# Windowed attention with a routed expert layer: transposing the probabilities in two row halves, and a new order of some loads and stores

## The chip, the cores and the metric

The kernel runs on one core of a Trainium2 chip. The core has four arithmetic engines that run side by side: TensorE (PE; its weight loads stand in a row of their own, PEld), VectorE (DVE), ScalarE (ACT) and GpSimd (POOL). SyncE (SP) only issues DMAs here. Sixteen DMA engines carry all transfers. The metric is the device time of one execution in microseconds (us); less is better. Times in the text are counted from the start of the profiled span.

## The reference

Attention in a window of 64 positions, over 8 batches, 8 heads, 576 positions and 64 dimensions a head, feeds a layer in which each token that passes a skip test goes through one of 8 experts:

```python
scores = q @ k.T / 8;  keep 0 <= i - j < 64, else -1e9
attn   = softmax(scores);  x = (attn @ v) as (4608, 512)
do     = x @ w_skip > 0;   e = argmax(x @ w_gate);  g = its softmax weight
out    = x;  out[do] = x + g * (relu(x @ w1[e]) @ w2[e])
```

## The kernel before

**Tiles.** The 4608 tokens are 36 tiles of 128, each made of two blocks of 64 positions. Nine tiles make a pair of batches: eight tiles with two neighbouring blocks of one batch, and a ninth, the tail tile, with the last block of either batch. For one tile TensorE writes 8 heads x 128 keys of scores into PSUM (`score`, line 252; line 238 adds the band mask). VectorE takes the row maximum and subtracts it (`lessen`, lines 267 and 268). ScalarE raises to e (`raise_e`, line 273) into s, 128 query rows by 8 x 128 keys. `transpose_p` turns each head's 128 x 128 probabilities over on TensorE (line 281), into two PSUM banks of four heads each, and ScalarE copies each bank into ptm (line 282). `av_tile` multiplies ptm by the values, their row sum and the gate columns (line 384). VectorE adds 1e-9 and takes the reciprocal (lines 395 and 396), scales into x (line 397) and into lh, the gate parts (line 403). In the last two tiles `into` hands `transpose_p` one score tile of two banks in place of two small ones.

**Order of the work.** The order on every engine is written by hand. Iteration t of the main loop issues, in this order: the loads due at t (`at`), the scores of tile t+1, gate matmuls (`gate_v`, line 331, which needs vT; `gate_vt`, line 339), `lessen` and `raise_e` of tile t, `tile_out` of tile t-2 (`av_tile` and its stores), `transpose_p` of tile t-1, and copies of values to the other half of the rows (`lower`). The routing of a group of 8 tiles (6 in two of them) is a generator, `route`, stepped by `routes` between those pieces. It puts small operations on GpSimd and VectorE, and matmuls (lines 513, 516 and 556) on TensorE, which may stand between a tile's value matmuls and its reciprocal. A score tile and the pt, pw and pk banks (tag "t") have two buffers, av has one, x has four.

**Queues.** SP issues loads and stores in program order, and a DMA takes one of eight semaphores in turn, so that an issue waits until the DMA eight before it has landed. `load_qk` (lines 210 and 211) brings the k and q of four tiles' worth of blocks, 1 MB, AHEADQ = 5 tiles ahead; `load_v` brings vT (line 292, 512 KB) and vm (line 298) AHEADV = 4 tiles ahead. `load_constants` (lines 176 and 177, 268 KB and 45 KB) is issued at the end of iteration 3, and `set_constants`, four small GpSimd operations that read them, at the end of iteration 5. A finished x is stored with a delay: `av_tile` appends it to `stores`, and `store` is called while more than SDELAY = 2 wait (in the last six tiles, while any waits). The store of an ordinary tile is one DMA of 128 rows (line 422); that of a tail tile is one DMA whose DRAM side has the shape 2 x 64 x 512 (line 425).

**After the loop** come the last transposes and value matmuls, mixed with the start of the expert layer. That layer is one long stream of float32r matmuls (lines 922 to 924), for which ScalarE and VectorE split the weights in a high and a low part (lines 848 and 852; the first three low parts on GpSimd). Tokens are gathered from and scattered to the output by indirect DMAs of GpSimd (lines 732 and 1025).

Of the kernel before, what the change touches and what calls it, by code (L numbers as in the profile page):

```python
# [8 lines left out]
F32 = mybir.dt.float32  # L9
# [9 lines left out]
B, H, S, HD = 8, 8, 576, 64  # L19
N, D, E, F = 4608, 512, 8, 1024  # L20
P = 128
NB = S // 64
NT = N // P
# [27 lines left out]
AHEADQ, AHEADV = 5, 4  # L51
SDELAY = 2
# [91 lines left out]
def window_attention_moe(ctx: ExitStack, tc, a, out):  # L144
    nc = tc.nc
# [6 lines left out]
    psum = ctx.enter_context(tc.tile_pool(name="psum", bufs=1, space=PSUM))  # L152
# [10 lines left out]
    ident = gid[:, 1]  # L163
# [67 lines left out]
    def score(t):  # L231

        ps = psc.tile([P, 2, 4, P], F32, name="ps")
        kinds = [min(i, 1) for _, i in tiles[t]]
        for hf in range(2):
            for r in range(2):
                h = slice(64 * r, 64 * r + 64)
                nc.tensor.matmul(
                    ps[64 * hf : 64 * hf + 64, r],
                    identb[h, h],  # L240
                    band[h, kinds[hf]].unsqueeze(1).to_broadcast([64, 4, P]),
                    start=True,
                    stop=False,
                    skip_group_check=True,
                )
        win = windows(t)
        for p in range(4):
            for hf in range(2):
                for r in range(2):
                    h = slice(64 * r, 64 * r + 64)  # L250
                    q, k = win[hf]
                    nc.tensor.matmul(  # L252
                        ps[64 * hf : 64 * hf + 64, r, p],
                        q[h, p],
                        k[h, :, p],
                        start=False,
                        stop=p == 3,
                        skip_group_check=True,
                    )
        ss[t] = ps  # L260

    def lessen(t):
        ps = ss[t]
        s = sp.tile([P, 2 * 4, P], F32, name="s")
        flat = ps.rearrange("p r h k -> p (r h) k")
        mx = sm.tile([P, 8], F32, name="mx", bufs=2)
        nc.vector.tensor_reduce(mx, flat, axis=AX.X, op=ALU.max)  # L267
        pace[0] = nc.vector.tensor_tensor(s, flat, mx.unsqueeze(2).to_broadcast([P, 8, P]), op=ALU.subtract)  # L268
        ss[t] = s

    def raise_e(t):
        s = ss[t]
        nc.scalar.activation(s, s, AF.Exp, scale=0.125)  # L273

    def transpose_p(t, into=None):
        s = ss.pop(t)
        ptm = ptp.tile([P, 8, P], F32, name="ptm")
        for r in range(2):
            pt = into[:, r] if into is not None else psum.tile([P, 4, P], F32, name="pt", tag="t", bufs=2)
            for p in range(4):  # L280
                nc.tensor.transpose(pt[:, p], s[:, 4 * r + p], ident)  # L281
            nc.scalar.copy(ptm[:, 4 * r : 4 * r + 4], pt)  # L282
        pts[t] = ptm

    ss, pts, vs = {}, {}, {}
# [32 lines left out]
    def keep_busy(n):  # L318

        idle = pav.tile([P, 2, 512], F32, name="av")  # L320
        for _ in range(n):
            nc.tensor.matmul(
                idle[:, 0], onesb, onesb.unsqueeze(1).to_broadcast([P, 4, P]),
                start=True, stop=True, skip_group_check=True,
            )
# [49 lines left out]
    def av_tile(t, lh, sums, av=None):  # L375
        blks = tiles[t]
        ptm, win = pts.pop(t), vs.pop(t)
        x = xp.tile([P, D], F32, name="x", bufs=XPB)
        if av is None:
            av = pav.tile([P, 2, 512], F32, name="av")  # L380
        banks["av"] = av
        for h in range(8):
            for hf in range(2):
                nc.tensor.matmul(  # L384
                    av[64 * hf : 64 * hf + 64, h // 4, (h % 4) * VW : (h % 4 + 1) * VW],
                    ptm[:, (h % 2) * 4 + h // 2, 64 * hf : 64 * hf + 64],
                    win[hf][:, h],
                    start=True,
                    stop=True,
                )  # L390
        if sums:
            sums()
        r = sm.tile([P, 2, 4], F32, name="r")
        src = av[:, :, : 4 * VW].rearrange("p z (h c) -> p z h c", c=VW)
        nc.vector.tensor_scalar(r, src[..., 64], 1e-9, None, op0=ALU.add)
        nc.vector.reciprocal(r, r)
        pace[0] = nc.vector.tensor_tensor(
            x.rearrange("p (z h c) -> p z h c", z=2, c=64),
            src[..., 0:64],
            r.unsqueeze(3).to_broadcast([P, 2, 4, 64]),  # L400
            op=ALU.mult,
        )
        nc.vector.tensor_tensor(  # L403
            lh.rearrange("p c (z h) -> p z h c", z=2),
            src[..., 65:74],
            r.unsqueeze(3).to_broadcast([P, 2, 4, 9]),
            op=ALU.mult,
        )
        if sums:
            sums()  # L410
        stores.append((x, blks))
        while len(stores) > (SDELAY if t < NT - 6 else 0):
            store()

    stores = []

    def store():
        x, ((b0, i0), (b1, i1)) = stores.pop(0)
        r0 = b0 * S + i0 * 64
        r1 = b1 * S + i1 * 64  # L420
        if r1 == r0 + 64:
            nc.sync.dma_start(out[r0 : r0 + P], x)
        else:
            both = out.rearrange("(b s) d -> b s d", s=S)[b0 : b1 + 1, i0 * 64 : i0 * 64 + 64]
            nc.sync.dma_start(both, x)

    def vector_part(t0, n, lh):
        lg = sm.tile([P, n, 9], F32, name="lg")
# [285 lines left out]
    def drip():  # L714
        if side:
            job = side.pop(0)
            if job:
                job[0](*job[1:])
# [28 lines left out]
    def clear_rows():  # L747
        for x in xgs:
            nc.gpsimd.memset(x, 0.0)
# [15 lines left out]
    def routes(n):  # L765

        for _ in range(n):
            for queue, h in ((late, held), (later, held2)):
                if not queue:
                    continue  # L770
                if h[0] in ("sums", "lists"):
                    h[1] += 1
                    if progress[0] < NT or h[1] < HOLD[h[0]] + (h is held2 and len(late)):
                        continue
                step(queue, h)

    def sums():
        step(late, held)
# [360 lines left out]
    first_of = [9 * (n // 4) + 2 * (n % 4) for n in range(NG)]  # L1139
    with tc.manual_schedule():  # L1140
# [16 lines left out]
        def when_at(t, f, n):  # L1157
            at.setdefault(max(t, 0), []).append((f, n))

        gate_at, lower_at, after_at = {}, {}, {}  # L1160
        for n in range(NG):
            if n >= 2:
                if n > 2:
                    when_at(first_of[n] - AHEADQ, load_qk, n)
                when_at(first_of[n] - AHEADV, load_v, n)
            gt = first_of[n] + 1 if n < 2 else first_of[n] - (2 if n > NSLOW else n == NSLOW)
            gate_at.setdefault(gt, []).append((gate_v, n))
            (after_at if n == 1 else gate_at).setdefault(gt + (n != 1), []).append((gate_vt, n))
            lower_at.setdefault(gt + 1, []).append((lower, n, 1))
            if n % 2:  # L1170
                lower_at.setdefault(gt + (1 if n == 3 else 2 * (n > 3)), []).append((lower, n, 0))
# [10 lines left out]
        for t in range(NT - 1):  # L1182
            m, r = divmod(t, 9)
            for f, n in at.get(t, ()):
                f(n)
            score(t + 1)
            gates = gate_at.get(t, ())
            if t == 0:
                keep_busy(5)
            for f, n in gates:  # L1190
                f(n)
            if t in (1, 2):
                transpose_p(t - 1)
            routes(1)
            if t != 3:
                lessen(t)
            raise_e(t)
            if t == 2:
                lessen(3)
            if BOTH <= t < NT - 2:  # L1200
                drip()
            if t >= 2:
                tile_out(t - 2)
            for f, n in after_at.get(t, ()):
                f(n)
            drip()
            routes(1)
            if t > 2:
                transpose_p(t - 1)
            if t == 1:  # L1210
                clear_rows()
            if t == 3:
                load_constants()
            if t == 5:
                set_constants()
            routes(1)
            for f, n, j in lower_at.get(t, ()):
                f(n, j)
            for _ in range(U0.count(t)):
                weight_dma_first()  # L1220
            if t == NT - 3:
                weight_hi(0)
# [197 lines left out]
    with tc.If(more > 0):  # L1420
        with tc.For_i(0, more, 1) as i:
# [15 lines left out]
            for qi in range(NQ):  # L1437
                both = []
                for w in range(2):
                    n = 2 * qi + w  # L1440
# [56 lines left out]
```

## Time and profile before

| | |
|---|---|
| Median of 3 runs | 412.88 us (412.46 to 413.97) |
| The profiled execution | 411.98 us |
| Its span | 410.2 us |
| TensorE, its weight loads, VectorE, ScalarE, GpSimd busy | 95%, 80%, 74%, 53%, 38% |
| Attention | about 0 to 161 us |
| Expert layer | about 159 us to the end |

The profile is one execution, taken by the hardware profiler. Busy shares are means over stages with different limits. A line of the timeline has a start and a length in us, and in square brackets the idle time of that engine before it with what ended it. The length of a batch of matmuls runs to the end of its last, and matmuls are pipelined, so a batch is shorter than the sum of its members. "128*128 128x128" behind a matmul gives rows and columns of the stationary operand, then the output. In "out<-a,b" the stationary operand is b.

### The profile page before, as it was taken

What the parts mean: (1) busy time and instruction counts of PE and PEld (TensorE: products, weight loads), DVE (VectorE), ACT (ScalarE), POOL (GpSimd) and SP (SyncE); (2) the same over time, 40 slices, a digit from 0 to 9 for tenths busy, and PEclk for the clock granted to TensorE, in tenths of its full rate; (3) what the DMA queues carried; (4) which work ended last, traced back from release to release, by engine and by line L of the source; (5) the groups of instructions that cost most, each with busy time, mean ns of one, the idle gap of its engine ahead of it and who ended that gap; (6) DMA issues with size and microseconds to landing.
All of it is one profiled execution on the core that took longest, in us unless ns stands there. A gap on an engine that the chain in (4) does not pass through costs nothing.

```text
span 410.2 us, 11472 instructions
## 1 busy us (share of the span) xinstructions
PE 390.3 (95%) x4624; PEld 326.4 (80%) x4624; DVE 303.2 (74%) x537; ACT 218.8 (53%) x373; POOL 154.2 (38%) x276
## 2 busy tenths in 40 slices
PE   8998899999999979899999999999999999999794
PEld 4776687877787768788888988988888888988673
DVE  3786789899989896999558699475366476758871
ACT  2775876866876796445234453343254435533450
POOL 5121358166658678985305032041034030100110
PEclk9999999999999999999999999999999999999998
DMA  8999999998996885747506959554236786641510
GB/s 300 406 384 381 410 409 297 405 409 319 335 413 243 288 298 202 259 164 229 175 2 192 343 175 290 177 173 153 91 124 216 259 273 203 237 150 55 195 38 22
DMA packets 34480, 99.41 MB, mean 242 GB/s; under 512 B 4248, under 2 KB 5528, under 8 KB 34424
## 3 DMA queue, kind: packets, MB, share of 16 engines
q1 hardware_dynamic: 30360, 87.30, 60.1%
q0 software_dynamic: 3200, 9.58, 6.8%
q10 hardware_dynamic: 864, 1.77, 1.1%
q8 instruction: 37, 0.61, 0.6%
q14 instruction: 19, 0.16, 0.1%
HBM read 84.57 MB, written 14.39 MB: 241 GB/s over the span
## 4 chain that ended last, share of the span: by engine, by line
PE 49%; issue 18%; DMA 13%; DVE 10%; ACT 5%; POOL 2%; SPq 1%; POOLq 0%; DVEq 0%
PE av L384 6%; DMA out<-yo,les 5%; PE p L922 5%; PE p L923 4%; PE p L924 4%; PE pt L281 4%; PE ps L252 4%; DVE s L268 3%; DMA raw<-wq 2%; DMA gid<-gid 2%; DMA kt<-kT 2%; PE pw L331 2%; DVE mx L267 2%; PE yv L922 2%; PE yv L923 2%
## 5 line engine op out<-in xcount | busy, mean ns | idle before, releaser
L852 DVE TENSOR_TENSOR wlo<-raw,whi 128x1024 fp32r<-128x1024 f32 x69 | 85.4, 1245 | 15.8 <-ACT whi L848 15.5
L985 ACT ACTIVATE hh<-p 128x256 fp32r<-128x256 f32 (+4 forms) x56 | 22.9, 409 | 98.0 <-PE p L924 93.8
L848 ACT CAST whi<-raw 128x1024 fp32r<-128x1024 f32 x72 | 74.4, 1045 | 0.0
L1025 POOL DMA_INDIRECT out<-yo,les x18 | 17.6, 976 | 145.9 <-DVE yo L1016 136.1
L922 PE MATMUL p<-xp,whi 128*128 128x256 f32 (+4 forms) x192 | 58.2, 303 | 1.0 <-DVE hl L988 1.0
L988 DVE SCALAR_TENSOR_TENSOR hl<-p,hh 128x256 fp32r<-128x256 f32 (+4 forms) x56 | 25.1, 450 | 45.0 <-ACT hh L985 33.3
L923 PE MATMUL p<-xp,whi 128*128 128x256 f32 (+4 forms) x192 | 57.0, 297 | 0.0
L924 PE MATMUL p<-xp,wlo 128*128 128x256 f32 (+4 forms) x192 | 56.8, 296 | 0.0
L273 ACT ACTIVATE s<-s 128x1024 f32<-128x1024 f32 x36 | 38.1, 1058 | 29.5 <-DVE s L268 29.2
L267 DVE TENSOR_REDUCE mx<-ps 128x8 f32<-128x1024 f32 x36 | 43.6, 1210 | 5.9 <-PE ps L252 5.9
L268 DVE TENSOR_TENSOR s<-ps,mx 128x1024 f32<-128x1024 f32 x36 | 44.1, 1225 | 4.8 <-PE pt L281 0.3
L384 PEld LDWEIGHTS av<-vm,ptm 128*64 128x64 f32 x992 | 34.3, 136 | 11.0 <-issue 6.2
L384 PE MATMUL av<-vm,ptm 128*64 128x74 f32 x992 | 39.0, 230 | 2.2 <-DVE lh L403 1.3
L922 PEld LDWEIGHTS p<-xp,whi 128*128 128x128 f32 x192 | 36.2, 188 | 3.7 <-DVE hl L988 1.4
L281 PE MATMUL pt<-gid,s 128*128 128x128 f32 x272 | 37.2, 279 | 0.1
L923 PEld LDWEIGHTS p<-xp,whi 128*128 128x128 f32 x192 | 36.2, 188 | 0.7
L282 ACT COPY ptm<-pt 128x512 f32<-128x512 f32 x68 | 36.2, 580 | 1.1 <-PE pt L281 0.6
L924 PEld LDWEIGHTS p<-xp,wlo 128*128 128x128 f32 x192 | 36.2, 188 | 0.0
L252 PE MATMUL ps<-k,q 64*64 64x128 f32 x1024 | 33.5, 269 | 0.0
L252 PEld LDWEIGHTS ps<-k,q 64*64 64x64 f32 x1024 | 30.2, 133 | 2.0
L281 PEld LDWEIGHTS pt<-gid,s 128*128 128x128 f32 x272 | 29.2, 141 | 3.1 <-issue 0.4
L353 POOL COPY vm<-vm 64x1184 f32<-64x1184 f32 (+1 forms) x17 | 18.8, 1108 | 31.0 <-ACT vm L351 27.5
(240 smaller groups left out, 823.7 us busy)
## 6 DMA issues: line engine op xcount, KB each, us to landing
raw<-wq SPq DMA_DIRECT2D x72, 512.0 KB, 4.9
vm<-vp SPq DMA_DIRECT2D x16, 592.0 KB, 8.6
out<-x SPq DMA_DIRECT2D x36, 256.0 KB, 8.3
vT<-vT SPq DMA_DIRECT2D x16, 512.0 KB, 8.3
q<-qT SPq DMA_DIRECT2D x13, 512.0 KB, 9.5
k<-kT SPq DMA_DIRECT2D x8, 640.0 KB, 9.0
k<-kT SPq DMA_DIRECT2D x7, 512.0 KB, 8.8
kt<-kT SPq DMA_DIRECT2D x8, 256.0 KB, 9.5
```

What stands on the lines that cost most here:

```text
L252: nc.tensor.matmul(ps[64 * hf : 64 * hf + 64, r, p], q[h, p], k[h, :, p], start=False, stop=p == 3, skip_group_check=True,)
L267: nc.vector.tensor_reduce(mx, flat, axis=AX.X, op=ALU.max)
L268: pace[0] = nc.vector.tensor_tensor(s, flat, mx.unsqueeze(2).to_broadcast([P, 8, P]), op=ALU.subtract)
L273: nc.scalar.activation(s, s, AF.Exp, scale=0.125)
L281: nc.tensor.transpose(pt[:, p], s[:, 4 * r + p], ident)
L282: nc.scalar.copy(ptm[:, 4 * r : 4 * r + 4], pt)
L384: nc.tensor.matmul(av[64 * hf : 64 * hf + 64, h // 4, (h % 4) * VW : (h % 4 + 1) * VW], ptm[:, (h % 2) * 4 + h // 2, 64 * hf : 64 * hf + 6 ...
L848: nc.scalar.copy(ring[n % RING][0], raw_of[n])
L852: by.tensor_tensor(lo, raw_of[n], hi.bitcast(F32), op=ALU.subtract)
L922: nc.tensor.matmul(o, lh, rh, start=first, stop=False, skip_group_check=parts)
L923: nc.tensor.matmul(o, lh, rl, start=False, stop=False, skip_group_check=parts)
L924: nc.tensor.matmul(o, ll, rh, start=False, stop=last, skip_group_check=parts)
```

## The change

`transpose_p` no longer turns a head over in one matmul. It takes the 64 upper and the 64 lower query rows of s apart: for each head two transposes of 64 rows by 128 keys, one behind the other, each with the matching 64 x 64 part of the identity. The upper halves of all heads go to one PSUM bank, the lower to another. Both copies into ptm come after the last transpose, and each writes 64 columns of every head.

A store is issued while more than one x waits, for the first eight tiles. The two blocks of a tail tile are stored by a DMA each. `load_constants` moves from iteration 3 to 7, `set_constants` from 5 to 10, and `load_qk` of group 4 from iteration 4 to 5.

```diff
-        for r in range(2):
-            pt = into[:, r] if into is not None else psum.tile([P, 4, P], F32, name="pt", tag="t", bufs=2)
-            for p in range(4):
-                nc.tensor.transpose(pt[:, p], s[:, 4 * r + p], ident)
-            nc.scalar.copy(ptm[:, 4 * r : 4 * r + 4], pt)
+        both = [
+            psum.tile([P, 8, 64], F32, name="pt", tag="t", bufs=2)
+            if into is None
+            else into[:, r].rearrange("p a (b c) -> p (a b) c", c=64)
+            for r in range(2)
+        ]
+        halves = [slice(64 * hf, 64 * hf + 64) for hf in range(2)]
+        for h in range(8):
+            for pt, q in zip(both, halves):
+                nc.tensor.transpose(pt[:, h], s[q, h], ident[q, q])
+        for pt, q in zip(both, halves):
+            nc.scalar.copy(ptm[:, :, q], pt)
...
-        while len(stores) > (SDELAY if t < NT - 6 else 0):
+        while len(stores) > (1 if t < 8 else SDELAY if t < NT - 6 else 0):
...
-            both = out.rearrange("(b s) d -> b s d", s=S)[b0 : b1 + 1, i0 * 64 : i0 * 64 + 64]
-            nc.sync.dma_start(both, x)
+            nc.sync.dma_start(out[r0 : r0 + 64], x[:64])
+            nc.sync.dma_start(out[r1 : r1 + 64], x[64:])
...
-                    when_at(first_of[n] - AHEADQ, load_qk, n)
+                    when_at(first_of[n] - AHEADQ + (n == 4), load_qk, n)
...
-            if t == 3:
+            if t == 7:
                 load_constants()
-            if t == 5:
+            if t == 10:
                 set_constants()
```

## Rows read from the trace of the kernel before

**Rows 1.** Windows: busy us (x instructions) of each engine, TensorE clock, DMA share, GB/s.

```profile
30.00:40.00 10.00, 8.57 (x186) 6.65 (x174) 6.51 (x13) 5.73 (x11) 1.91 (x5) 1.00 1.02 376
...
54.00:58.00 4.00, 4.00 (x92) 3.10 (x88) 3.68 (x8) 2.82 (x6) 1.53 (x6) 1.00 1.03 409
...
66.00:70.00 4.00, 4.00 (x90) 3.16 (x86) 3.80 (x6) 2.24 (x5) 3.83 (x5) 1.00 0.92 245
...
280.00:320.00 40.00, 40.00 (x264) 34.64 (x263) 20.30 (x27) 16.19 (x33) 8.41 (x7) 1.00 0.45 148
```

**Rows 2.** Lines, VectorE, 48.3 to 150.2 us: busy, mean ns | idle before, releasers.

```profile
L395 DVE TENSOR_SCALAR r<-av 128x8 f32<-128x8 f32 x25 | 4.0, 160 | 3.5 <-PE av L556 2.2 <-PE av L516 0.6 <-PE av L384 0.5
```

**Rows 3.** Lines by form, TensorE, whole span, same columns.

```profile
L384 PE MATMUL av<-vm,ptm 128*64 128x74 f32 x992 | 39.0, 230 | 2.2 <-DVE lh L403 1.3 <-issue 0.9
...
L281 PE MATMUL pt<-gid,s 128*128 128x128 f32 x272 | 37.2, 279 | 0.1
```

**Rows 4.** Timeline, one tile: start us, length us, engine, line, form, count, idle before.

```profile
88.38 1.09 PE L281 MATMUL pt<-gid,s 128*128 128x128 f32 x8
...
89.64 1.04 PE L252 MATMUL ps<-k,q 64*64 64x128 f32 x32
...
89.77 1.05 ACT L282 COPY ptm<-pt 128x512 f32<-128x512 f32 x2
...
91.19 1.25 PE L384 MATMUL av<-vm,ptm 128*64 128x74 f32 x32
```

**Rows 5.** The same transposes with 80 rows: timeline, and line by form.

```profile
249.25 0.44 PE L895 MATMUL px<-gid,xg 80*128 80x80 f32 x4
...
L895 PE MATMUL px<-gid,xg 80*128 80x80 f32 x4 | 0.4, 231 | 0.0
```

**Rows 6.** Timeline of SP, TensorE, GpSimd and VectorE, 26 to 39 us.

```profile
26.19 0.33 SPq L176 DMA_DIRECT2D cf<-c_f  x1
...
30.30 0.38 SPq L292 DMA_DIRECT2D vT<-vT  x1
...
31.90 0.29 POOL L180 CAST trib<-cf 128x128 bf16<-128x128 f32 x1 [3.42 <-DMA cf<-c_f]
...
33.42 0.51 SPq L422 DMA_DIRECT2D out<-x  x1
...
35.40 0.69 DVE L397 TENSOR_TENSOR x<-av,r 128x512 f32<-128x512 f32 x1 [2.85 <-DMA out<-x]
...
38.99 1.07 PE L252 MATMUL ps<-k,q 64*64 64x128 f32 x32
```

**Rows 7.** Chain of waits: start us, length us, what.

```profile
29.85 5.45 DMA out<-x
...
46.02 0.57 PE pw L331 x8
...
74.61 0.57 PE pw L331 x8
```

**Rows 8.** Landing, vT load of 30.30 and store of 33.42, in that order.

```profile
DMA to landing us min/median/max: 6.5/6.5/6.5
...
DMA to landing us min/median/max: 9.2/9.2/9.2
```

**Rows 9.** Timeline of TensorE and VectorE, last tiles of the attention.

```profile
151.06 0.66 PE L281 MATMUL ps<-gid,s 128*128 128x128 f32 x4 [0.59 <-ACT s L273]
...
153.21 0.66 PE L281 MATMUL ps<-gid,s 128*128 128x128 f32 x4 [1.49 <-ACT ptm L282]
...
155.35 0.17 DVE L395 TENSOR_SCALAR r<-av 128x8 f32<-128x8 f32 x1 [1.80 <-PE av L516]
...
158.75 0.66 PE L281 MATMUL ps<-gid,s 128*128 128x128 f32 x4 [0.73 <-ACT ptm L282]
```

**Rows 10.** Waits of SP: total us, times, longest.

```profile
SPq L292 <- DMA out<-x: 7.7, 2, 4.1
```

**Rows 11.** Timeline of SP, that vT load's issue.

```profile
65.08 0.33 SPq L292 DMA_DIRECT2D vT<-vT  x1
```

## The prediction

> **What bounds the kernel now.** I read the windows first, then the chain of waits, then the lines of VectorE (DVE) for one long stretch, then single stretches of the timeline. In the windows the reader is to see two kinds of time. From 280 to 320 us, in the expert part, TensorE is busy 40.00 of 40 us with DMA at 0.45 [rows 1]: there every microsecond by which the attention ends sooner is a microsecond of the whole. In the attention the other engines are near their limit as well. From 30 to 40 us TensorE is busy only 8.57 of 10 while DMA stands at 1.02 [rows 1]: something other than arithmetic sets the pace there. From 48.3 to 150.2 us, 25 tiles in 101.9 us, VectorE waits for TensorE for no more than 3.5 us in all, before line 395, in front of the reciprocal [rows 2]. So in this long middle TensorE and VectorE are almost equally late, and a faster TensorE can win 3.5 us at most, whatever it saves.
>
> **The transposes.** Removed: 8 transposes a tile, each with a stationary operand of 128 rows and 128 columns and 128 streamed columns. Added: 16, in 8 pairs, each of 64 rows and 128 columns with 64 streamed columns, the two of a pair in different halves of the rows and different PSUM banks. The old rhythm: a batch of 8 takes 1.09 us [rows 4], one of them 0.28 us [rows 3], so (1.09 - 0.28) / 7 = 0.116 us from one to the next. Does such a rhythm go with the columns loaded or with those streamed? The transposes of 80 rows load the same 128 columns and stream 80: four take 0.44 us, one 0.231 [rows 5], hence 0.070. Rhythm goes with streamed columns, and a load of 128 columns costs at most 0.070. Do two row halves run side by side? The score matmuls do: 32 of them, in fours over two row and two column halves, 128 columns streamed, take 1.04 us [rows 4], so with a last one of about 0.27 a four takes (1.04 - 0.27) / 7 = 0.110. But these load 64 columns each; two loads of 128 columns in two row halves stand nowhere in the trace. Bounds for a pair: 64 / 128 of 0.110 = 0.055 from below; 2 x 0.070 = 0.140 from above, loads one after another. The nearest row is that of the value matmuls, 16 pairs in two column halves, 74 columns streamed, in 1.25 us [rows 4] with 0.230 for one [rows 3]: 0.068 a pair. I take 0.068. A tile's transposes then cost 8 x (0.116 - 0.068) = 0.38 us less of TensorE (bounds: 0.49 less, 0.19 more).
>
> The Trainium skill, "TensorE: Matmul & The Clock Gate", section "LDWEIGHTS (loading the stationary operand)", speaks against this: a load takes its columns divided by 1.2 in nanoseconds, however few rows it has. By that figure two loads of a pair, one after the other, would take an estimated 0.213 us and lengthen the kernel by over 20 us; the transposes of 80 rows at 0.070 us disagree with the 0.107 us that it gives for one load [rows 5].
>
> The middle takes of the 0.38 us a tile only what VectorE waits. Of the 3.5 us, 2.2 us come in three tiles in which the list matmuls of line 556 stand ahead of the reciprocal [rows 2]; those tiles keep 0.7 - 0.38 = about 0.35 each, some 1.1 us together, and the rest goes. Gain 2.3 us (0 to 3.5). What is late next is VectorE itself. The copies into ptm both start after the last transpose now, where the first used to start after four of eight; ScalarE runs them only behind the tile's exponential anyway, two in 1.05 us from 89.77 when the transposes had started at 88.38 [rows 4], so this costs nothing while that cover stands. Without it the cost is one copy, about 0.5 us a tile. The rows into which the copies write are now runs of 64 instead of 512 elements; I give that nothing, and at most a tenth of a copy, which the same cover hides.
>
> **The end of the attention.** The last two tiles transpose into one score tile, and there the second four wait for the copy of the first four: 1.49 us at 153.21 and 0.73 us at 158.75 [rows 9]. Now no copy is issued between the transposes, so both waits go. The value matmuls of tile 33, which stand behind those transposes on TensorE, can then start as soon as their own copies are done, and the reciprocal that waits 1.80 us at 155.35 [rows 9] follows at once. The 0.59 us at 151.06, for the exponential, stays. The next thing late is the low half of the first expert weights on GpSimd, which stays where it is behind two gathers; I take 2.1 of the 2.22 us for that reason (1.0 to 2.2).
>
> **The stores and loads at the start.** At 35.40 VectorE has waited 2.85 us to write the fifth x [rows 6]: its buffer is the first x, whose store was issued at 29.85 and took 5.45 us [rows 7]. SP now issues that store one iteration sooner, in the place of the constants, which went at 26.19 [rows 6]. With the same 5.45 us it lands at 31.6, and the wait goes; the second store follows it. The DMA engines are full here, so the order of the bytes decides what is late next. By their shapes two stores (512 KB) go ahead of the batch's k and q in place of 313 KB of constants: k and q land later by 199 KB at 376 GB/s [rows 1], 0.5 us. That q was issued just before the vT load of 30.30, which took 6.5 us [rows 8], so it was there by 36.8 at the latest; its first use came at 38.99 [rows 6] and comes at about 35.5 now: from no wait to 1.8 us. The vT of the next batch pair sets the firmer limit. It was issued just behind the store of 33.42 [rows 6], which took 9.2 us [rows 8], so it landed at 43 to 44, and its gate matmuls stood at 46.02 [rows 7]. The bytes ahead of it are the same to 60 KB. So of 2.85 us, and of what the faster transposes add, 2 to 3 us can be kept at that point: 2.3 us (0.5 to 3.0).
>
> The constants wait behind the fifth store now. set_constants on GpSimd, which idled 3.42 us for them at 31.90 [rows 6], is issued five iterations later, when they have long landed; its four operations, under a microsecond, lie ahead of routing work that has several tiles of slack. Cost nothing; without the slack, 1 us once.
>
> **The tail result in two stores.** From 54 to 58 us the DMA engines move 409 GB/s, from 66 to 70 us, after the first such store, 245 [rows 1]; SP waits up to 4.1 us for such a store before it can issue a vT load [rows 10], at 65.08 [rows 11]. Its gate matmuls stand at 74.61 [rows 7]. With the gain so far they come near 70, and with a landing of 6.5 us [rows 8] the load would be there only at 71.6: 1.6 us would be lost. The Trainium skill, "DMA: Bandwidth & Descriptors", section "Why a DMA increments its semaphore by 16 and not by 1", says that the slowest dimension of either side limits how many of the 16 DMA engines share a transfer; that dimension is 2 in the old store and 64 in the new. The fall to 245 GB/s agrees with it. So I give this edit no gain, but without it I would take 1.6 us off. It adds four issues on SP of about 0.35 us, which idles between issues.
>
> **The sum.** 2.3 + 2.3 + 2.1 = 6.7 us. The profiled execution took 411.98 us (span 410.2), 0.9 us under the median of the runs, 412.88. 411.98 - 6.7 = 405.3 for such an execution, 406.2 for a median.
>
> **Rivals.**
> A. The two loads of a pair follow each other: 0.110 to 0.140 us a pair. For it: no row has two such loads. Against it: in the score matmuls four loads share 0.110 us. The start and the end keep their 4.4 us, the middle gains nothing, at 0.140 it loses 0.19 us in 34 tiles, 6.5 us: 408.5 to 415.
> B. The loads are what is late at the start: q or vT makes TensorE wait for what the store no longer does, DMA being full. The start gains 0.5 instead of 2.3 and the middle starts later: 408.0 (407 to 409.5). For it: 1.02 of DMA [rows 1]; against it: the vT had 2 to 3 us to spare.
> C. Slower: a load of half the rows costs as much as a whole old transpose, 0.110, and the two of a pair do not overlap, 0.220 a pair. Place: TensorE, every tile, (0.220 - 0.116) x 8 = 0.83 us in 34 tiles = 28 us, less 4.4: 437. It decides from the point where a pair takes more than 0.116 + 4.4 / (8 x 34) = 0.132 us. The rule on loads above is this rival's page; the transposes of 80 rows speak against it.
> D. The halves run side by side but nothing follows in the middle, because the chain exponential, copies, value matmuls is as long as VectorE's own: 408.5. This is the near end of my own range.
>
> **How the numbers follow.** Forecast with D 0.64 (403.5 to 408.7 its own range), A 0.15, B 0.13, C 0.08. Under 0.5%, 2.06 us, this kernel cannot be told from no change, so faster means under 410.8, slower over 414.9. Faster: the forecast 0.64, B 0.12, A 0.07, together 0.83; same: A 0.05 and B 0.01; slower: C 0.08 and the upper end of A 0.03. The range 402.5 to 411.5 holds the forecast, B and the lower half of A, about 0.85, and leaves out C and A's upper end.
>
> **What would show it.** The batch of 16 transposes should take about 0.75 us in the timeline (0.65 to 0.85; 1.1 or more is A, 1.8 is C). Line 397 should have no wait for out<-x; the gate matmuls that stood at 46.02 should come at about 43.7. The waits of the transposes for ptm in the last tiles should be gone, and VectorE's waits at the reciprocal in the middle fall from 3.5 to about 1 us. After the tail stores DMA should stay near 400 GB/s. The first expert matmul and the end should both come 6.7 us sooner. The forecast is wrong if the first has moved by less than 4 us, or if it has and the end has not.

## The result and the profile after

The kernel after takes 415.25 us (median of 12 runs, 414.14 to 418.27), the kernel before 412.55 us beside it (12 runs, 412.02 to 414.37): 1.0062 times as long, 95% interval 1.0044 to 1.008. The forecast was 406.2 us, so its sign was wrong. The profiled execution took 414.31 us (span 412.5).

First the page: busy time by engine, the chain of waits by engine, and the line of ScalarE that the change touches.

```profile
PE 384.4 (93%) x4912; PEld 320.0 (78%) x4912; DVE 303.9 (74%) x537; ACT 218.0 (53%) x373; POOL 153.4 (37%) x276
...
issue 38%; PE 27%; DVE 11%; POOL 11%; DMA 8%; ACT 4%; POOLq 1%; DVEq 0%; SPq 0%
...
L289 ACT COPY ptm<-pt 128x512 f32<-128x512 f32 x68 | 36.1, 582 | 5.3 <-PE pt L287 5.1
```

TensorE is busy 6 us less than before (390.3) and has 288 matmuls and 288 weight loads more. "Issue", time in which the engine waited for nothing that the profile shows, is 38% of the chain; it was 18%. A copy into ptm takes 582 ns, where it took 580. The first expert matmul starts at 161.16 us, where it started at 159.16. The same windows as in [rows 1], and VectorE's reciprocal over the same stretch as in [rows 2]:

```profile
30.00:40.00 10.00, 8.16 (x204) 6.70 (x204) 7.02 (x12) 6.97 (x12) 0.95 (x1) 1.00 1.01 375
54.00:58.00 4.00, 3.74 (x90) 2.80 (x88) 3.23 (x8) 3.17 (x5) 2.41 (x9) 1.00 1.01 399
66.00:70.00 4.00, 2.92 (x74) 2.22 (x68) 3.93 (x7) 2.53 (x4) 3.37 (x11) 1.00 1.03 404
280.00:320.00 40.00, 40.00 (x255) 34.03 (x253) 21.01 (x27) 15.53 (x32) 8.63 (x8) 1.00 0.42 142
```

```profile
L402 DVE TENSOR_SCALAR r<-av 128x8 f32<-128x8 f32 x25 | 4.0, 161 | 5.0 <-PE av L391 3.4 <-PE av L563 1.0 <-PE av L523 0.4
```

From 66 to 70 us DMA moves 404 GB/s instead of 245, but TensorE is idle 1.08 of 4 us in a place where it was never idle. VectorE waits longer at the reciprocal, 5.0 us against 3.5, though TensorE has less to do. The timeline of TensorE (start, length, instruction, idle time before it and what ended it) shows what the idle time is:

```profile
66.47 0.34 PE L287 MATMUL pt<-gid,s 64*128 64x64 f32 x3
67.89 0.59 PE L287 MATMUL pt<-gid,s 64*128 64x64 f32 x13 [1.08 <-issue]
...
71.53 0.71 PE L287 MATMUL pt<-gid,s 64*128 64x64 f32 x16
...
72.42 0.61 PE L252 MATMUL ps<-k,q 64*64 64x128 f32 x16
74.14 0.67 PE L252 MATMUL ps<-k,q 64*64 64x128 f32 x16 [1.12 <-issue]
...
78.61 0.80 PE L391 MATMUL av<-vm,ptm 128*64 128x74 f32 x17
80.47 0.73 PE L391 MATMUL av<-vm,ptm 128*64 128x74 f32 x15 [1.07 <-issue]
```

A batch of 16 transposes takes 0.71 us where nothing interrupts it, as forecast (0.75). But at 66.58, 72.75 and 79.18 TensorE stops in the middle of a batch: after 3 of 16 transposes, after 16 of 32 score matmuls, after 17 of 32 value matmuls. These instructions wait for no semaphore. Counted from the start of the last instruction before to the start of the next, there are twelve such stops of 0.3 to 1.6 us, 10.2 us in all, between 22 and 154 us, nine of them before 81 us. The kernel before has none in mid-batch after 10 us.

The packets of the DMA queue called "instruction" go with them. The page has its packets, MB and share (37 packets before):

```profile
q8 instruction: 39, 0.64, 0.6%
```

Each has 16,384 bytes. Start and end of four of them, read from the same trace, in us:

```
packet starts   packet ends   TensorE goes on   from the last "goes on" to the start
   65.34           66.42          67.88
   71.64           72.70          74.14                 3.76
   78.28           79.25          80.47                 4.14
   82.34           83.30        (no stop)               1.87
```

All twelve stops end 1.2 to 1.6 us after a packet has landed, and the ends of three in a row are 6.26 and 6.33 us apart. Their place tells more. Number all of TensorE's records in the trace (matmuls, weight loads and the few of its sequencer) from 0 on: from 20 us to the end of the attention, every stop of 0.4 us or more that waits for no semaphore, in this kernel and in all the experiments below, stands ahead of a record whose number leaves 193 when divided by 256, whatever instruction that is. So my theory: TensorE's instructions, 256 to a packet, are fetched by the same DMA engines that move the data. While these are full, the next 256 are usable only about 6.2 us after TensorE has begun the present ones. Its pace is then bounded at 256 / 6.2 = 41 instructions a microsecond, whatever they do. The Trainium skill, "Runtime: NRT & Kernel Launch", section "Instruction fetch mechanics", says that an engine's sequencer fetches blocks of 16 KiB, 256 instructions, over a DMA queue of its own while the block before is executed; the packets here agree in size and number: 9,824 weight loads and matmuls make 38.4 blocks.

The time of each tile's x tells where the microseconds went (start of the multiplication that writes x, us from the start of the span; e1 to e11 are the experiments below):

```
                       tile 0   tile 4   tile 14   tile 31   tile 34
before                  17.46    35.40    76.85    146.56    162.50
after                   18.30    35.10    81.68    150.19    164.53
split only      (e1)    18.67    37.18    81.16    153.05    166.79
moves only      (e2)    18.06    33.15    74.67    144.42    160.35
fillers         (e3)    17.98    35.68    80.91    155.20    173.68
split from 14   (e4)    18.31    33.44    75.52    148.38    161.37
split from 31   (e5)    17.80    33.01    74.63    144.63    158.78
three at a time (e8)    18.29    36.54    87.82    172.89    186.94
split from 33   (e9)    17.86    32.98    74.92    145.06    159.11
split from 34  (e10)    17.86    32.85    74.47    144.20    158.50
stores sooner  (e11)    17.72    32.71    76.14    145.88    163.30
```

After loses 4.8 us to before by tile 14, holds most of that to tile 31, and wins 1.6 back at the end of the attention. The differences at tile 0, up to 1.2 us, come from one execution each; I don't explain them.

### The profile page after: what moved, and what is told of

Same layout as the page of the kernel before. It is cut to its first block, busy times and chain, and to the rows that moved or that the text cites. A ratio compares the mean times of both kernels' runs of the same rounds, so it can differ in the third digit from the quotient of the medians.

```text
span 412.5 us, 12062 instructions
## 1 busy us (share of the span) xinstructions
PE 384.4 (93%) x4912; PEld 320.0 (78%) x4912; DVE 303.9 (74%) x537; ACT 218.0 (53%) x373; POOL 153.4 (37%) x276
## 4 chain that ended last, share of the span: by engine, by line
issue 38%; PE 27%; DVE 11%; POOL 11%; DMA 8%; ACT 4%; POOLq 1%; DVEq 0%; SPq 0%
PE av L391 7%; DMA out<-yo,les 5%; PE ps L252 4%; POOL xg L739 4%; DVE s L268 3%; PE pt L287 2%; POOL out L1032 2%; DVE mx L267 2%; PE pw L338 2%; POOL wlo L859 2%; DVE x L404 2%; PE ps L238 1%; DMA out<-x 1%; PE av L329 1%; ACT ptm L289 1%
## 5 line engine op out<-in xcount | busy, mean ns | idle before, releaser
L1032 POOL DMA_INDIRECT out<-yo,les x18 | 17.6, 977 | 146.8 <-DVE yo L1023 137.1
L391 PEld LDWEIGHTS av<-vm,ptm 128*64 128x64 f32 x992 | 35.6, 136 | 13.2 <-issue 8.2
L391 PE MATMUL av<-vm,ptm 128*64 128x74 f32 x992 | 41.3, 231 | 3.6 <-issue 2.7
L252 PE MATMUL ps<-k,q 64*64 64x128 f32 x1024 | 35.3, 270 | 3.2 <-issue 3.2
L252 PEld LDWEIGHTS ps<-k,q 64*64 64x64 f32 x1024 | 31.2, 133 | 6.3 <-issue 4.3
L287 PE MATMUL pt<-gid,s 64*128 64x64 f32 x544 | 25.1, 229 | 2.0 <-issue 1.1
L929 PE MATMUL yv<-whi,hh 128*128 128x512 f32 x64 | 25.9, 405 | 0.0
```

The lines of the kernel that those rows point to most:

```text
L252: nc.tensor.matmul(ps[64 * hf : 64 * hf + 64, r, p], q[h, p], k[h, :, p], start=False, stop=p == 3, skip_group_check=True,)
L287: nc.tensor.transpose(pt[:, h], s[q, h], ident[q, q])
L391: nc.tensor.matmul(av[64 * hf : 64 * hf + 64, h // 4, (h % 4) * VW : (h % 4 + 1) * VW], ptm[:, (h % 2) * 4 + h // 2, 64 * hf : 64 * hf + 6 ...
L929: nc.tensor.matmul(o, lh, rh, start=first, stop=False, skip_group_check=parts)
```

## Experiments

**Which part loses: e1, e2.** Rivals to the theory: the moved stores and loads make early data late (1), or the halves lengthen every tile (2). e1 takes the new `transpose_p` alone, e2 all the rest.

```diff
 # e1: the kernel before
-        for r in range(2):
-            pt = into[:, r] if into is not None else psum.tile([P, 4, P], ...)
...
+        for h in range(8):
+            for pt, q in zip(both, halves):
+                nc.tensor.transpose(pt[:, h], s[q, h], ident[q, q])
 # e2: the kernel after, with these lines the other way round
```

> The kernel before with the transposes in two halves of rows and nothing else of the change. Theory (TensorE's instructions arrive too late while the DMA engines are saturated: 256 of them in about 6.3 us, and the split asks for 16 more a tile): TensorE stops of 0.3 to 1.6 us in the middle of a batch, with no semaphore waited for, return between 20 and 80 us, some 8 us in all, and the time is 413 to 416 us. Rival 1 (the moved stores and loads are what made the early tiles late): no such stops, 406 to 409 us. Rival 2 (the halves themselves, their two copies waiting for all sixteen transposes, lengthen every tile): the loss is spread over all 36 tiles, 413 to 416 us, with waits of copies and of row maxima instead of stops without a semaphore.

Measured: 416.47 us (6 runs), 1.008 of before (1.0058 to 1.0103). Stops without a semaphore are back, twelve of 0.28 to 1.8 us, 12.3 us in all, now as far as 128 us. Three of them in the timeline of TensorE:

```profile
43.38 0.43 PE L252 MATMUL ps<-k,q 64*64 64x128 f32 x4 [1.06 <-issue]
...
79.95 0.73 PE L391 MATMUL av<-vm,ptm 128*64 128x74 f32 x15 [1.07 <-issue]
...
122.08 0.65 PE L252 MATMUL ps<-k,q 64*64 64x128 f32 x10 [1.22 <-issue]
```

> The kernel after with the old transposes of 128 rows; stores, constants, q and k and the tail stores stay moved. Theory (instruction supply): no stop of TensorE over 0.25 us in mid-batch without a semaphore, 410.5 to 413 us. Rival 1 (moves make data late): 414 to 417 us, with waits for loads before 80 us. Rival 2 (halves lengthen every tile): 410.5 to 413 us as well.

Measured: 410.25 us, 0.9943 (0.992 to 0.9965). No stop in mid-batch after 10 us. So rival 1 falls: the moves gain, and the split alone loses at least about as much as the whole change. TensorE from 10 to 80 us, first e2, then the kernel after (busy us and instruction counts of TensorE, its weight loads, VectorE, ScalarE, GpSimd; clock, DMA share, GB/s):

```profile
10.00:80.00 70.00, 69.02 (x1402) 54.18 (x1405) 61.04 (x106) 54.14 (x93) 25.85 (x50) 1.00 1.03 403
```

```profile
10.00:80.00 70.00, 60.01 (x1397) 46.16 (x1396) 56.36 (x95) 49.62 (x85) 24.68 (x49) 1.00 1.03 395
```

This pair is the heart of the case. In 70 us TensorE executes the same number of instructions, 1402 and 1397 matmuls, in one kernel busy 69.02 us and in the other 60.01. The work per instruction became less, the instructions per microsecond did not become more. VectorE shows the price: 95 operations in place of 106. The nine stops up to 81 us are 8.7 us together, nearly all of the 9.0 us by which TensorE is busy less.

That also leaves little to rival 2. From 48.3 to 150.2 us VectorE's row maxima wait for nothing (line 267, 0.0 us idle) in the kernel after as before. From 10 to 160 us TensorE's gate matmuls and copies of values (pw, pk) wait 1.8 us for copies into ptm, where they waited 1.2. Such waits exist, but they are small beside the stops.

**More instructions without the split: e3.** Sixteen more TensorE instructions a tile, in the kernel before.

```diff
         banks["av"] = av
+        for _ in range(8):
+            nc.tensor.matmul(av[0:64, 1, 480:512], onesb[:64, 0:64], onesb[:64, 0:32], ...)
```

> The kernel before with eight small bfloat16 matmuls (64 rows, 32 columns, into an unused corner of the av bank) ahead of each tile's av matmuls: 16 more TensorE instructions a tile, as many as the split adds, and nothing of the change itself. Theory (instruction supply): stops of 0.3 to 2 us without a semaphore appear between 20 and 80 us, hardly any after 80 us; the tiles before 80 us become longer by 0.3 to 0.6 us more than the tiles after it; 418 to 430 us in all, the fillers' own time included. Rivals 1 and 2: no such stops, the tiles before and after 80 us grow alike by the fillers' own 0.3 to 0.5 us.

Measured: 422.88 us (one run). Stops appear with the old transposes:

```profile
30.06 0.80 PE L389 MATMUL av<-vm,ptm 128*64 128x74 f32 x17 [0.43 <-issue]
...
43.09 0.62 PE L331 MATMUL pw<-vT,gid 128*32 128x256 f32 x2 [0.59 <-issue]
```

Three of them, 2.0 us, all before 44 us. The halves are thus not needed for a stop. The second half of what I expected did not come: up to tile 14 a tile grew by 0.25 us, from tile 14 to 30 by 0.27 (x of tile 30 at 151.17 against 142.79). The reason lies in the experiment: the fillers take TensorE's time as well and lengthen the tile by themselves. The packets start 6.21 us apart in e3 (mean from 20 to 80 us) and 6.20 in e2. Where nothing stops, this spacing is only the pace at which TensorE asks: in e2 each packet lands 1.6 to 2.3 us before TensorE comes to the place of the stops. So e3 tells that added instructions alone make stops, not what the split costs.

**The disputed cost by itself: e6.** A stream of TensorE instructions, without and beside loads.

```diff
+        stream(768)      # transposes of 64 rows, in two row halves, no data moving
+        small(768)       # bfloat16, 64 rows, 32 columns, no data moving
...
+        for i, z in enumerate(big):   # 40 loads of 512 KB
+            nc.sync.dma_start(z, a["wq"][r : r + P, c : c + 1024])
+        stream(512)
+        small(640)
```

> Nothing of the reference is computed: a stream of TensorE instructions alone, 768 transposes of 64 rows and 768 small bfloat16 matmuls with no data moving, then 512 and 640 of them beside 20 MB of loads (some 50 us) that don't feed them. Theory (instruction supply): without loads no stop over 0.25 us, though 256 instructions take 5.6 us as transposes and less as small matmuls, or stops with a period clearly under 6.3 us; beside the loads one stop for each line of 256 instructions, the lines 6.0 to 6.6 us apart, whatever the instructions are. Rival (the supply has a fixed pace, with or without loads): the same spacing in both stretches. Rival (there is no such limit): no stops in either, 5.6 us for 256 instructions of transposes in both.

Windows of transposes without loads, of transposes and small matmuls beside loads, and of small matmuls alone beside them, then the timeline of both stretches of transposes:

```profile
6.00:28.00 22.00, 22.00 (x692) 22.00 (x691) 0.00 (x0) 0.00 (x0) 0.00 (x0) 1.00 0.01 4
...
74.00:97.00 23.00, 17.93 (x493) 17.35 (x490) 0.00 (x0) 0.59 (x1) 0.00 (x0) 0.90 1.03 410
97.00:128.00 31.00, 28.80 (x540) 28.69 (x538) 0.00 (x0) 0.00 (x0) 0.00 (x0) 0.50 1.03 406
```

```profile
2.64 26.20 PE L125 MATMUL pt<-ident,s 64*128 64x64 f32 x768 [2.64 <-DMA ident<-gid]
...
68.69 8.51 PE L125 MATMUL pt<-ident,s 64*128 64x64 f32 x223 [2.44 <-ACT s L147]
77.97 4.25 PE L125 MATMUL pt<-ident,s 64*128 64x64 f32 x128 [0.77 <-issue]
84.16 5.64 PE L125 MATMUL pt<-ident,s 64*128 64x64 f32 x128 [1.94 <-issue]
90.36 1.28 PE L125 MATMUL pt<-ident,s 64*128 64x64 f32 x33 [0.55 <-issue]
...
96.55 13.62 PE L130 MATMUL av<-onesb 64*64 64x32 bf16 x252 [1.81 <-issue]
```

With DMA at 0.01, 768 transposes, each with its load, run without a stop in 26.20 us: 256 instructions in 4.4 us (I had expected 5.6). Beside the loads (DMA 1.03) it executes 128 matmuls, with their loads exactly 256 instructions, stops, and goes on at 77.97, 84.16, 90.36 and 96.55: 6.19, 6.20 and 6.19 us apart. That the last of these blocks is partly of other matmuls changes nothing. The stream has no data to wait for and reads none of what is loaded. Both rivals (a fixed pace, no limit) fall. From 97 us on the granted clock is 0.50, 252 matmuls take 13.62 us, so a block takes longer than 6.2 us, and there are no stops.

**Where the split may stand: e4, e5, e9, e10.** The kernel after, with the old transposes for the first tiles.

```diff
+        if t < 14:       # e4;  NT - 5 in e5, NT - 3 in e9, NT - 2 in e10
+            (the eight transposes of 128 rows)
+        else:
             (the sixteen of 64 rows)
```

> The kernel after with the old transposes for the first 14 tiles and the split ones from tile 14 on. Theory (instruction supply): no stops before 70 us, x of tile 14 within 1 us of its time in the kernel before (76.9 us from the span's start, 81.7 in the kernel after), the gain of the later tiles kept (2 to 3 us): 408.5 to 411 us, faster than both. Rival 1: as the kernel after, 414 to 416 us. Rival 2: about half of the loss stays, 412.5 to 414.5 us.

Measured: 410.75 us, 0.9932 (0.9907 to 0.9957). The 4.8 us lost by tile 14 are gone (x at 75.52), but the gain of the later tiles is not there: one stop at 35.9 us, with old transposes, and seven between 84 and 144 us, two of them:

```profile
85.16 0.66 PE L252 MATMUL ps<-k,q 64*64 64x128 f32 x13 [0.73 <-issue]
...
143.86 1.47 PE L252 MATMUL ps<-k,q 64*64 64x128 f32 x31 [1.89 <-issue]
```

The stops went where the split went. I had taken the later tiles to be free of them, because the kernel after has only three from 81 us on; that part of the expectation failed. By the intervals e4 is no better than e2.

> The moved stores and loads with the old transposes for the first 31 tiles and the split ones for the last five alone. Theory (instruction supply): no stop of TensorE without a semaphore in the attention, the 2.2 us that the moves gave (x of tile 14 at 74.7 us), and 2 to 3 us between x of tile 31 and x of tile 34, as the kernel with late splits had (12.99 us there, 15.94 before): 407 to 409 us, faster than every kernel so far. Rival (the gain of the late splits was only the filling up of a loss made just before): 15 to 16 us between these two x, 410 to 411 us.

Measured: 408.99 us, 0.9895 (0.9865 to 0.9925): faster than before and after. Tile 31 to 34 takes 14.15 us, where e2 takes 15.93. I had expected no stop, but one of 0.6 us at 141.2 and one of 1.9 us at 146.8 are left. The first expert matmul comes at 155.38, in e2 at 157.01:

```profile
148.62 0.61 PE L398 MATMUL av<-vm,ptm 128*64 128x74 f32 x12 [1.63 <-issue]
...
155.38 0.39 PE L936 MATMUL p<-xh,whi 128*128 128x256 f32 x1
```

> As the kernel with five split tiles at the end, with the last three alone split. Theory (instruction supply): 32 instructions fewer between 140 and 150 us, so the stop of 1.86 us that stood at 146.8 us there goes or shrinks; the waits for the copies of ptm at the end are saved as well: 407 to 409.5 us. If the stop stays (the weight loads at 140 to 150 us are enough by themselves): 408.5 to 410 us.

Measured: 410.29 us, 0.9926 (0.9889 to 0.9963). The stop of 1.9 us is gone, and one of 0.3 us at 142.2 is left, but x of tile 34 is no earlier, and the time is a little over the range I gave.

> The last two tiles alone split, whose transposes have banks of their own. Theory: the 2.2 us that TensorE waited for copies of ptm there go (1.49 and 0.73 us before): 407.5 to 409.5 us. Rival (the end of attention isn't bound by these waits): 410 to 411 us, as with the moves alone.

Measured: 409.66 us, 0.9907 (0.9879 to 0.9934), just over the range; tile 31 to 34 takes 14.30 us. The waits for ptm are most of the gain at the end. The intervals of e5, e9 and e10 overlap, and each of them overlaps that of e2: which is best, and by how much they pass the moves alone, these times don't tell. The earlier x of tile 34 is what speaks for the split there.

**The start: e11.** The kernel before with the sooner stores alone.

```diff
-        while len(stores) > (SDELAY if t < NT - 6 else 0):
+        while len(stores) > (1 if t < 8 else SDELAY if t < NT - 6 else 0):
```

> The kernel before with one edit, the stores of the first eight tiles one tile sooner. Forecast of the prediction for the start: VectorE no longer waits 2.85 us for the store of x ahead of tile 4, which gives 2.3 us: 410 to 411.5 us, x of tile 4 near 33.1 us. Rival (the moved constants and q and k are what freed the start): 412 to 413.5 us, x of tile 4 near 35 us.

Measured: 412.67 us (12 runs), 0.9979 (0.9952 to 1.0006), in the range that I gave to the rival, and not told from no change. The trace says more. VectorE's x of tile 4, then TensorE's gate matmuls:

```profile
32.72 0.69 DVE L397 TENSOR_TENSOR x<-av,r 128x512 f32<-128x512 f32 x1
```

```profile
45.24 0.64 PE L331 MATMUL pw<-vT,gid 128*32 128x256 f32 x8 [1.90 <-DMA vT<-vT]
```

The 2.85 us of [rows 6] are gone at tile 4, and 1.90 of them are given back at the gate, which waits for its vT. In e2 the same gate stands at 43.76 with no wait. Both theories had a half: the stores free VectorE, and the constants and k and q, by standing behind, let the vT come in time to keep it. Which of these other moves does it, no run shows.

**Fewer transfers under way: e8.** The kernel after, the transfers of the attention on SyncE's queue each waiting for the third before it. The loads of q in `load_qk` were left out of this, so more than three can be under way.

```diff
+        if len(line) > 20:
+            tc.add_manual_dep(ins.ins, line[-3].name, info, reason="in turn")
```

> The kernel after, with every load and store of the attention on SyncE's queue, from the twenty-first on, waiting until the third before it has landed, so that at most three are under way. Theory (instruction supply, late because many packets stand ahead of it): the stops before 80 us become shorter or go; what is gained is lost in part where data come later: 411 to 416 us. Rival (the fetch waits only for its share of a busy engine, not behind a queue): stops as in the kernel after as long as the DMA engines stay busy, 415 to 420 us. If the DMA engines fall idle in between and the stops stay, the loads don't cause them.

Measured: 436.59 us, 1.053 (1.0478 to 1.0582). From 40 to 80 us:

```profile
40.00:80.00 40.00, 31.18 (x715) 24.30 (x713) 29.66 (x54) 25.74 (x45) 18.68 (x43) 0.96 0.87 286
```

One stop is left there, 0.9 us (6.9 us in the kernel after between 40 and 81 us), but TensorE now waits 15.3 us for vT up to 190 us and asks for instructions more slowly. So it does not tell whether the depth of the queue or the load of the engines delays the fetch.

## Why the prediction was wrong

**The transposes: the duration right, the gain not.** A pair costs 0.068 us and the batch 0.71; rivals A and C did not occur. The step that failed is "The middle takes of the 0.38 us a tile only what VectorE waits. ... Gain 2.3 us (0 to 3.5)". Its lower bound of 0 takes it that less time on TensorE cannot hurt. The sixteen added instructions a tile were priced by their time on the engine and nowhere as instructions that have to be fetched. At 6.2 us for 256, as in e6, one costs 24 ns while DMA is full: fifteen tiles of 16 make 240, an estimated 5.8 us up to tile 14. Measured, after against e2 at tile 14: 81.68 - 74.67 = 7.0 us. The sum had +2.3 in the place of that.

The pace was to be had from the trace of before, the limit was not. Its packets of the instruction queue start at 46.72, 52.91, 58.83, 64.57, 71.42, 77.83 and 83.99: 6.2 us apart, the spacing that e6 shows to be the limit, without one stop. Each lands 2.8 to 3.8 us before TensorE comes to the place of the stops, while every stop of these runs ends within 1.6 us of a landing. So the kernel before asked for instructions at the pace of the limit, with a reserve; that it was the limit, only e6 tells. And "something other than arithmetic sets the pace there", read off [rows 1], was followed up for the stores alone.

**From tile 14 on** after wins 2.8 us on before: 1.6 from tile 31 to 34, the rest, 1.2, from tile 14 to 31. But in that stretch e1, with the same split, takes 2.2 us more than before, and e4 3.1 us more than e2. So these runs don't show a gain of the split in the middle; part of the 1.2 may only be the catching up of the late start.

**The end of the attention: right.** The waits for ptm of [rows 9] are gone. The batches into the score tile stand in the timeline of after unbroken and without a wait for copies:

```profile
154.71 0.69 PE L287 MATMUL ps<-gid,s 64*128 64x64 f32 x16
...
160.06 0.71 PE L287 MATMUL ps<-gid,s 64*128 64x64 f32 x16
```

Tile 31 to 34 takes 15.94 us before, 14.34 after, 14.15 in e5: 1.6 to 1.8 us; I took 2.1 (1.0 to 2.2).

**The start: right in size.** e2 is 2.25 us ahead at tile 4 and 2.15 to 2.2 all the way to the end; I took 2.3. In after most of it drowns in two stops at 22.7 and 29.1 us (1.7 us). For the later constants the prediction has "Cost nothing", and they cost nothing; but without them and the other moves e11 gives 1.9 us back at the gate, so the gain of the start is one of the moves together. Its gate matmuls came at 43.76 in e2, as forecast (43.7).

**The tail stores: the rate as forecast, the price not shown.** There is no fall to 245 GB/s from 66 to 70 us: 404 in after, 416 in e2, where the rate stays at 392 to 416 from 54 to 82 us. Whether 1.6 us would have been lost without this edit, no run shows. From x of tile 34 to the end of the span it is 247.70 us before and 247.75 in e2, so the expert part neither gains nor loses, as [rows 1] had it.

**The rivals.** None named the mechanism. D, "nothing follows in the middle", was the nearest: it had 0 there, with another cause, and from tile 4 to tile 31 the kernel after takes 3.9 us more than before (115.09 against 111.16).

## What to carry to other kernels

Count instructions as well as microseconds: where DMA stands at 1.0, an edit that trades long instructions for more short ones can lose, here an estimated 24 ns for each one added. Before you trust a cheaper instruction mix, look in the instruction queue at the spacing of the packets and at how long before it is needed each one lands, and read a stop in mid-batch marked "issue", 1.2 to 1.6 us behind the landing of a packet, as a fetch that came late. Put such an edit where the transfers have room or where it removes a wait (here the last tiles), which with the moved stores gave 408.99 us.

## What the runs showed of the hardware

- Every stop of 0.4 us or more without a semaphore stands at the same place in 256 TensorE records, and ends 1.2 to 1.6 us after a packet of 16,384 bytes on the instruction queue has landed.
- TensorE gets 256 instructions per 6.19 us beside full DMA (share 1.03), and at least 256 per 4.4 us without (e6).
- After some of the longer stops in the attention the granted clock fell: in e1 after 1.8 us at 28.9 us to 0.50 from 32 to 34 us, in e4 after 2.16 us at 141.7 us to 0.53 from 146 to 148 us, in e8 after 1.55 us at 28.5 us to 0.50 from 31 to 34 us, that is from the higher of its two levels, 2.4 GHz, to the lower, 1.2 GHz. A stop then costs more than its own length; in e4 32 value matmuls took 2.24 us instead of 1.25. After the stops of 1.86 us in e5 and 1.63 us in the kernel after it stayed at 1.00.
- Two loads of 128 columns in two row halves, with their transposes, take 0.068 us a pair.
- Open: why stops in the kernel after are rare from 81 to 150 us and are not in e1 and e4, and whether they follow the load of the DMA engines or the number of packets that wait. The share of DMA alone does not decide it: it is 1.03 from 10 to 80 us both in e2, without a stop, and in the kernel after, with nine.
